# A four-stage attention and expert kernel on one core: stash copies in runs of four, a fixed matmul order for the first expert, weight loads on another queue

## The chip, the cores and the metric

The kernel runs on one core of a Trainium2 chip. The metric is device time in microseconds, the median of several executions. One execution was also profiled; its rows are what the text reads. The engines are named as in the profile: PE (matrix multiply) with PEld (its weight loads), DVE (vector), ACT (scalar), POOL (GpSimd) and SP (it issues DMAs). ACT and POOL can issue DMAs too; an issue stands in the engine's own instruction stream, in order. Each engine executes its instructions in the order in which the program laid them down; that order is decided before the run.

## What is computed

The reference chains three layers over 3072 tokens of width 384 (4 batches of 768 steps, 8 heads of 48).

```
for t in range(S):                      # gated linear attention, complex decay a
    S_re, S_im = a_t * (S_re, S_im) + (k_t v_t^T, 0)
    y_t = q_t @ S_re
e = argmax(x @ w_gate); do = x @ w_skip > 0
x = x + do * gate * relu(x @ w1[e]) @ w2[e]      # 8 experts, 384 -> 1024 -> 384
out = leaky(x @ w_in) @ w_out                    # 384 -> 2048 -> 384, leaky = max(0.01 h, h)
```

## The kernel before

The batches are handled in two halves, unit 0 and unit 1. For each unit the work has four parts.

**Rows.** `attention_rows` holds one sequence chunk of 96 steps in every partition row (128 rows: 2 batches, 8 heads, 8 chunks). It normalises `a` (`norm_pre`, `norm`), forms the running products `P` step by step on DVE (`steps`: one multiply into `t`, one add into `P`, each needing the last), and scales k and q by them (`scaled_pre`, `scaled`). Steps come in blocks (`BLKA` for unit 0, mostly 8 steps; `BLKB` for unit 1, mostly 6). For unit 0 the results stay in SBUF: `turned` transposes four steps of k or q at a time into one PSUM bank (`qkps`, 96 partitions by 4 steps by 128 rows) and ACT copies that bank into the `stash`, whose innermost dimension is the step. `timed` writes the order of DVE, ACT and PE in this part out by hand. A few ACT operations of the last blocks are given to POOL by the lists `GUARD_G` and `MIRROR_G`. For unit 1 the results go through a DRAM tensor `kqd`; this generator is called `behind` and is fed piecemeal into later parts.

**Chunks.** `attention_chunks` does scores, outputs and states per chunk on PE, then `Routing` selects 128 slots per expert.

**Experts.** `experts` runs eight experts for the unit. For each, `columns` transposes the gathered tokens, `first` does 48 matmuls into `hps` with four ReLUs (`hh`) on ACT, `second` does 16 matmuls into `yps`, and DVE adds (`xo`) before a scatter to `xd`. For unit 0 the weights are whole fp32 and lie in the stash: those of experts 0 to 3 come during the chunks, those of experts 4 to 7 by `fetch` into slots that an earlier expert's matmuls have finished reading. After each of the four groups of `first`, `go` calls `budget(behind, 2.0)` while `e < LASTE`: it emits background work (the generator `feed`) until its planned microseconds are used up, with DVE and ACT kept in program order. After expert 3's `first`, `swap` frees half of the stash and adds to `feed` the conversion of `w_in` (`convert`): 16 pieces, each loaded as raw 64-bit words (`raw`, two buffers), turned into fp32 on DVE (`cst`, three operations), split by ACT (high half, into `m2w`) and DVE (low half). `feed` takes one item from `behind` and one from the conversion in turn.

**Dense.** `Dense` does the two wide layers for 512 tokens at a time: `load` reads `xd` (tile `xr`), `columns` transposes, `first` gives `hps`, `second` gives `ops`. In the first of them the conversion of `w_out` runs as background work, in the next the rest of `behind`. Then unit 1 goes through chunks, experts and dense in the same way, with its expert weights converted to fp16 pairs.

Where nothing is kept in program order, a list scheduler orders the instructions of each engine by its own estimate of when they become ready.

Of the kernel before, what the change touches and what calls it, by code (L numbers as in the profile page):

```python
# [11 lines left out]
I32 = mybir.dt.int32  # L12
I64 = mybir.dt.int64
# [6 lines left out]
B, H, S, D = 4, 8, 768, 48  # L20
# [28 lines left out]
BG_START = 1.5  # L49
BG_CHUNK = 0.3  # L50
BG_ROUTE = 12.0
BG_EXPERT, LASTE = 2.0, 6
BG_DENSE = (1, 1.5, 1.5)
BG_WOUT = 0.3
BG_WSTART, BG_WEIGHT = 4.0, 0.35
# [11 lines left out]
SUM_NORM = (0, 1, 2)  # L67
SUM_SCALED = (12, 13)
MIRROR = (0, 1)
GUARD_G = (10, 11, 13)  # L70
MIRROR_G = (11, 12, 13)
LISTS = dict(sp=(0, 1), tp=(2, 3, 7), yps=(4,), ups=(5,), tr=(6,), bk=(7,))
DEEP = {"kqt": 3, "vt": 3, "qT": 3}
LISTSA = dict(sp=(0, 1), yps=(2,), ups=(3,), tr=(4, 5, 6), bk=(7,))
# [4 lines left out]
def moe_attention_kernel(ctx, tc, q, k, v, a_re, a_im, w_skip, w_gate, w1, w2, w_in, w_out, out,  # L79
                         cap=CAP):  # L80
    nc = tc.nc
# [13 lines left out]
    V, A, T, G = Engine(nc.vector, "V"), Engine(nc.scalar, "A"), Engine(nc.tensor, "T"), Engine(nc.gpsimd, "G")  # L95

    def keep(engines):
        for n in order:
            order[n] = n in engines
# [50 lines left out]
    def rows3(x):  # L150
        return x.rearrange("(k p) f -> p k f", p=128)


    def attention_rows(ui, ep, blks, sum_pe, queue, store, stash=None, more=None):
# [31 lines left out]
        a4s, Ps, ins, pre, turns, lags = {}, {}, {}, {}, [], []  # L186
# [24 lines left out]
        def norm_pre(i):  # L211
# [14 lines left out]
            A.activation(rr, r0, AF.Square)  # L226
            if stash and i in GUARD_G:
                G.tensor_scalar(s2, r0, 0.5e-6 / MAGCAP, -0.5, ALU.mult, ALU.add)
# [4 lines left out]
        def norm(i):  # L233
# [21 lines left out]
            for c in range(2):  # L255
                if stash and i in MIRROR_G and not c:
                    G.tensor_scalar(a4[:, :, 3 - 2 * c, :], a4[:, :, 2 * c, :], 1.0 - 2 * c, None, ALU.mult)
# [21 lines left out]
        def scaled(i):  # L279
# [30 lines left out]
            if stash:  # L310
                turns.append(turned(i, kq))
            else:
                queue.dma_start(kqd[t0s[i]:t0s[i] + blks[i]].rearrange("t r a d -> r t (a d)"),
                                kq[2].rearrange("r t a c d -> r t (a c d)"))
            yield cost(i, 2)

        def turned(i, kq):

            for g in range(0, blks[i], 4):
                m = min(4, blks[i] - g)  # L320
                for a in range(2):
                    p = ps.tile([2 * D, m, R], F32, tag="qk", name="qkps")
                    for j in range(m):
                        T.transpose(p[:, j, :], kq[a][:, g + j].rearrange("p c d -> p (c d)"), ident)
                    t = t0s[i] + g
                    lags.append((stash[a][:2 * D, :, :, t:t + m].rearrange("p c b t -> p t (c b)"), p))
                    if len(lags) > 1:
                        A.activation(*lags.pop(0), AF.Copy)
                    yield
# [461 lines left out]
    def convert(pool, src, hi, lo, scale, cut, shape, n):  # L791

        raw, t = {}, {}
        el = 1
        for d in shape:
            el *= d
        cost = (70 + 1.04 * el) / 1e3
        for j in range(n + 1):  # L800
            if j:
                A.activation(hi[cut(j - 1)], t[j - 1], AF.Copy, scale=scale)
            if j < n:
                r = pool.tile([128] + shape + [2], I32, tag="raw", name="raw")
                nc.sync.dma_start(r.rearrange("p k f w -> p k (f w)").bitcast(I64), rows3(src)[cut(j)])
                t[j] = pool.tile([128] + shape, I32, tag="cst", name="cst")
                V.tensor_scalar(t[j], r[:, :, :, 1], 0x07FFFFFF, 3, ALU.bitwise_and, ALU.logical_shift_left)
                yield 0.6 * cost
                V.scalar_tensor_tensor(t[j], r[:, :, :, 1], -0x40000000, t[j], ALU.bitwise_and, ALU.bitwise_or)
                yield cost  # L810
                V.scalar_tensor_tensor(t[j], r[:, :, :, 0], 29, t[j], ALU.logical_shift_right, ALU.bitwise_or)
                t[j] = t[j].bitcast(F32)
                yield cost
            else:
                yield 0.0
            if j:
                V.scalar_tensor_tensor(lo[cut(j - 1)], t[j - 1], scale, hi[cut(j - 1)], ALU.mult, ALU.subtract)
                yield cost
# [3 lines left out]
    def cut_columns(m, n):  # L822
        return lambda j: (al, al, slice(j * m // n, (j + 1) * m // n))

    def cut_rows(m, n):
        return lambda j: (al, slice(j * m // n, (j + 1) * m // n))
# [12 lines left out]
    class Experts:  # L839
# [2 lines left out]
            self.ui, self.whole, self.place = ui, whole, place  # L842
            self.w, self.xg, self.xt, self.h, self.slots, self.made = {}, {}, {}, {}, [], 0

        def weights(self, e, layer, half):

            src, k, m = ((w1[e], 3, F1), (w2[e], 8, DM))[layer]
            t = self.w[e, layer] = self.place(e, layer).rearrange("p (k m) -> p k m", k=k)
            c = (al, al, slice(half * m // 2, (half + 1) * m // 2)) if layer == 0 else \
                (al, slice(half * k // 2, (half + 1) * k // 2))  # L850
            nc.scalar.dma_start(t[c], rows3(src)[c])

        def part(self, i):

# [96 lines left out]
    class Dense:  # L951
# [4 lines left out]
        def load(self):  # L956
            self.xr = self.xp.tile([128, 4, DM], F32, tag="xr", name="xr", bufs=1)
            nc.sync.dma_start(self.xr, xd[self.ui][self.t * TN:(self.t + 1) * TN, :]
                              .rearrange("(s p) c -> p s c", p=128))
# [43 lines left out]
    def run(*gens):  # L1003
        for gen in gens:
            for _ in gen:
                pass
# [3 lines left out]
    def budget(gen, us, engines=""):  # L1010

        was = "".join(n for n in order if order[n])
        keep(engines)
        owed[0] += us
        while owed[0] > 0:
            x = next(gen, None)
            owed[0] = 0.0 if x is None else owed[0] - x
        keep(was)

    def later(us, gen):  # L1020

        for _ in range(int(us * 10)):
            yield 0.1
        for x in gen:
            yield x
# [127 lines left out]

    def experts(ex, behind, us, then={}, mixed=none):

        ex.columns(0)
        for e in range(E):
            gen = none if ex.place else ex.made_to(2 * e + NSLOT, ex.stage)
            if e in (() if ex.place else MIX):
                next(mixed, None)  # L1160

            def go():
                for _ in range(3):
                    next(gen, None)
                budget(behind, us if e < LASTE else 0.0, "VA")

            for _ in ex.first(e):
                go()
            then.get((e, 0), list)()
            if e + 1 < E:  # L1170
                ex.columns(e + 1)
            run(gen)
            ex.second(e)
            then.get((e, 1), list)()
# [7 lines left out]
    stash = [p.tile([128, NCH, HB * H, L], F32, name="stash") for p in blocks]  # L1182
# [25 lines left out]
    ex = Experts(0, range(E), place)  # L1208

    def fetch(*which):  # L1210
        def go():
            for e, layer in which:
                for half in range(2):
                    ex.weights(e, layer, half)
        return go

    chunks_and_routing(ck[0], rt, later(BG_START, behind), BG_CHUNK,
# [11 lines left out]
    feed = share(behind)  # L1229
    mlp2 = {}  # L1230

    def swap():
        blocks[1].release()
        wpm = mlp2["w"] = tc.alloc_tile_pool(name="wpm", bufs=1)
        mlp2["x"] = tc.alloc_tile_pool(name="m2x", bufs=2)
        cp = mlp2["c"] = tc.alloc_tile_pool(name="cp", bufs=2)
        for i, (shape, src, scale, cut, part) in enumerate((
                ([128, 3, F2], w_in, SWI, cut_columns(F2, CVP), [3, F2 // CVP]),
                ([128, 16, DM], w_out, SWO, cut_rows(16, CVP), [16 // CVP, DM]))):
            t = mlp2[i] = [wpm.tile(shape, F16, name=f"m2w{i}{j}") for j in range(2)]  # L1240
            mlp2["conv", i] = convert(cp, src, *t, scale, cut, part, CVP)
        feed.gens.append(mlp2["conv", 0])

    then = {(i // 2, i % 2): fetch((i // 2 + 2, i % 2)) for i in range(8, 12)}
    then.update({(i, 1): fetch((4 + i // 2, i % 2)) for i in range(4)})
    then[3, 0] = swap
    experts(ex, feed, BG_EXPERT, then=then)
    (wih, wil), (woh, wol), m2x = mlp2[0], mlp2[1], mlp2["x"]
    conv = mlp2["conv", 1]
# [22 lines left out]
    ex = Experts(1, ())  # L1272
# [5 lines left out]
    conv = later(BG_WSTART, ex.made_to(4, ex.stage))  # L1278
# [15 lines left out]
    conv = ex.made_to(NSLOT, ex.stage)  # L1294
# [3 lines left out]
    run(conv)  # L1298
    rest = second_ff(dense[ND:nd], True)
    experts(ex, none, 0.0, mixed=rest)  # L1300
    dense[nd].load()
    run(rest)
# [139 lines left out]
```

## Time and profile before

| | us |
|---|---|
| median of 3 runs | 952.55 (951.84 to 953.05) |
| the profiled execution | 956.44 |
| its span, first to last instruction | 954.0 |
| PE busy | 840.4 |
| DVE busy | 612.4 |
| ACT busy | 518.0 |
| POOL busy | 137.2 |

By the trace the parts of unit 0 lie at about 0 to 151 us (rows), 151 to 249 (chunks and routing), 249 to 372 (experts) and 372 to 514 (two dense tiles); unit 1 follows to the end. Busy shares are averages over parts with different limits, so the rows below are taken by stretch.

### The profile page before, as it was taken

To read this page: it belongs to the slowest core of one execution; us is meant where nothing else is said; L and a number is where in the kernel's file an instruction comes from. 1 tells how busy PE (TensorE), PEld (TensorE's weight loads), DVE (VectorE), ACT (ScalarE), POOL (GpSimd) and SP (SyncE) were. 2 spreads that over 40 slices of the span, in tenths; PEclk is the share of its full clock that TensorE was granted. 3 is DMA by queue.
4 is the path that set the end of the run, shared out by engine and by line. 5 is a ranking of instruction groups with operands and counts; after the bars stand their busy time and mean duration, and the time that the engine had idled before them with its cause. 6 is when DMAs were issued, how large, how long until landed. Compare 5 with 4: busy or idle time off the path is not lost.

```text
span 954.0 us, 17829 instructions
## 1 busy us (share of the span) xinstructions
PE 840.4 (88%) x6674; PEld 584.8 (61%) x6674; DVE 612.4 (64%) x1534; ACT 518.0 (54%) x1065; POOL 137.2 (14%) x168
## 2 busy tenths in 40 slices
PE   1787878899299783999999988999999999999997
PEld 1665667898288572455457978846776645546454
DVE  6978884677788579999961555587577262260430
ACT  4879896676255343654743867655566261350430
POOL 9100022221541012000012111140011000000000
PEclk9979897999599986999999989999999999999999
DMA  5555544898668876445246898242766201000000
GB/s 152 143 152 159 139 114 144 243 290 268 200 206 276 283 271 217 147 134 172 78 156 165 224 234 241 75 162 86 246 201 214 88 1 51 18 1 25 9 10 27
DMA packets 126512, 143.61 MB, mean 151 GB/s; under 512 B 34058, under 2 KB 109514, under 8 KB 126416
## 3 DMA queue, kind: packets, MB, share of 16 engines
q1 hardware_dynamic: 106064, 107.88, 38.5%
q10 hardware_dynamic: 18304, 29.89, 9.6%
q0 software_dynamic: 2048, 4.61, 1.4%
q8 instruction: 54, 0.88, 0.4%
q14 instruction: 42, 0.34, 0.1%
HBM read 115.62 MB, written 28.41 MB: 151 GB/s over the span
## 4 chain that ended last, share of the span: by engine, by line
PE 55%; DVE 16%; DMA 14%; ACT 10%; issue 3%; SPq 1%; ACTq 0%; POOL 0%; DVEq 0%; POOLq 0%
PE ops L91 17%; PE hps L91 13%; PE yps L91 7%; PE sps L91 4%; DVE gg L91 3%; DMA raw<-in_moe_w_in_dram 3%; DVE gl L91 3%; DVE cst L91 2%; PE ad L91 2%; ACT stash L91 2%; PE tps L91 2%; ACT gh L91 2%; DMA kqt<-kqd 2%; PE ups L91 2%; DMA cw<-in_moe_w_dram 2%
## 5 line engine op out<-in xcount | busy, mean ns | idle before, releaser
L91 PE MATMUL hps<-xTh,m2w 128*128 128x512 f16 x576 | 174.1, 381 | 0.6 <-issue 0.3
L91 PEld LDWEIGHTS <-m2w 128*128 128x128 f16 x864 | 84.5, 98 | 100.7 <-issue 3.9
L91 PE MATMUL ops<-m2w,gh 128*128 128x384 f16 x512 | 125.2, 326 | 0.0
L91 PE MATMUL hps<-xTl,m2w 128*128 128x512 f16 x288 | 109.4, 381 | 0.1
L91 DVE TENSOR_TENSOR gg<-hps,gg 128x512 f32<-128x512 f32 x96 | 65.8, 685 | 65.5 <-ACT gg L91 65.1
L91 PE MATMUL ops<-m2w,gl 128*128 128x384 f16 x256 | 83.5, 326 | 0.0
L91 ACT ACTIVATE ot<-ops 128x384 f32<-128x384 f32 x24 | 11.6, 489 | 121.2 <-PE ops L91 121.2
L91 PEld LDWEIGHTS <-gh 128*128 128x128 f16 x512 | 50.1, 98 | 32.7
L91 DVE TENSOR_TENSOR t<-P,a 128x192 f32<-128x192 f32 x190 | 66.8, 352 | 1.3 <-ACT a L91 0.4
L91 PE MATMUL ops<-m2w,stash 128*128 128x384 f16 x384 | 65.3, 326 | 1.8 <-ACT m2w L91 1.8
L91 ACT ACTIVATE gg<-hps 128x512 f32<-128x512 f32 x96 | 56.3, 586 | 17.5 <-PE hps L91 12.4
L91 DVE TENSOR_TENSOR gl<-gg,gh 128x512 f16<-128x512 f32 x64 | 44.2, 690 | 33.6 <-ACT gh L91 33.3
L91 DVE SCALAR_TENSOR_TENSOR w<-cw,w 128x768 f16<-128x768 f32 x64 | 59.8, 953 | 7.7 <-ACT w L91 7.2
L91 ACT ACTIVATE gh<-gg 128x512 f16<-128x512 f32 x64 | 40.3, 630 | 43.2 <-DVE gg L91 42.9
L91 ACT ACTIVATE w<-cw 128x768 f16<-128x768 f32 x64 | 53.0, 844 | 17.9 <-DMA cw<-in_moe_w_dram 15.4
L91 POOL TENSOR_SCALAR_AFFINE_SELECT sc<-sc 96x384 f32<-96x384 f32 x64 | 34.6, 550 | 157.6 <-ACT sc L91 157.2
L91 PEld LDWEIGHTS <-stash 128*128 128x128 f16 x384 | 37.5, 98 | 29.2 <-issue 4.8
L91 POOL DMA_INDIRECT xd<-xo,idx x16 | 25.2, 1574 | 179.9 <-DVE xo L91 166.1
L91 ACT ACTIVATE stash<-qkps 96x512 f32<-96x512 f32 (+1 forms) x50 | 50.0, 1025 | 0.4 <-PE qkps L91 0.4
L91 DVE TENSOR_TENSOR P<-t 128x96 f32<-128x96 f32 x190 | 48.5, 255 | 1.6
L91 PE MATMUL yps<-stash,hh 128*128 128x384 f32 x128 | 44.7, 503 | 3.8 <-ACT hh L91 3.8
L91 ACT ACTIVATE hh<-hps 128x256 f32<-128x256 f32 (+1 forms) x64 | 23.8, 378 | 40.6 <-PE hps L91 28.7
(245 smaller groups left out, 1779.6 us busy)
## 6 DMA issues: line engine op xcount, KB each, us to landing
stash<-in_moe_w_dram ACTq DMA_DIRECT2D x32, 768.0 KB
cw<-in_moe_w_dram SPq DMA_DIRECT2D x64, 384.0 KB
kqt<-kqd SPq DMA_DIRECT2D x16, 576.0 KB
kqd<-kq SPq DMA_DIRECT2D x14, 576.0 KB
vd<-gv SPq DMA_DIRECT2D x32, 192.0 KB
vt<-vd SPq DMA_DIRECT2D x32, 192.0 KB
raw<-in_moe_w_in_dram SPq DMA_DIRECT2D x16, 384.0 KB
raw<-in_moe_w_out_dram SPq DMA_DIRECT2D x16, 384.0 KB
```

What stands on the lines that cost most here:

```text
L91: ins = getattr(self.engine, op)(*args, **kw)
```

## The change

Six edits. The stash copies walk the bank with the step innermost, so that four consecutive stash elements are written one after another, and PSUM is read with a step of 128 elements. The lists that gave six operations to POOL are empty, so ACT does them. In `experts` of unit 0, PE keeps program order from the first expert's `columns` until the second's. The weights that `fetch` loads are issued by SP in place of ACT. `convert` issues the load of a piece before the work on the piece ahead of it, and the first load already in `swap`. The conversion of `w_in` now goes ahead of `behind` in the feed instead of in turn with it, and the background budget runs to expert 6 instead of expert 5.

```
-BG_EXPERT, LASTE = 2.0, 6
+BG_EXPERT, LASTE = 2.0, 7
-GUARD_G = (10, 11, 13)
-MIRROR_G = (11, 12, 13)
+GUARD_G = ()
+MIRROR_G = ()
...
-                    lags.append((stash[a][:2 * D, :, :, t:t + m].rearrange("p c b t -> p t (c b)"), p))
+                    lags.append((stash[a][:2 * D, :, :, t:t + m].rearrange("p c b t -> p (c b) t"),
+                                 p.rearrange("p t r -> p r t")))
...
+        def load(j):
+            raw[j] = pool.tile([128] + shape + [2], I32, tag="raw", name="raw")
+            nc.sync.dma_start(raw[j].rearrange("p k f w -> p k (f w)").bitcast(I64), rows3(src)[cut(j)])
+
+        load(0)
+        yield 0.0
         for j in range(n + 1):
+            if j + 1 < n:
+                load(j + 1)
             if j:
                 A.activation(hi[cut(j - 1)], t[j - 1], AF.Copy, scale=scale)
             if j < n:
-                r = pool.tile([128] + shape + [2], I32, tag="raw", name="raw")
-                nc.sync.dma_start(r.rearrange("p k f w -> p k (f w)").bitcast(I64), rows3(src)[cut(j)])
+                r = raw.pop(j)
...
-        def weights(self, e, layer, half):
+        def weights(self, e, layer, half, queue=nc.scalar):
...
-            nc.scalar.dma_start(t[c], rows3(src)[c])
+            queue.dma_start(t[c], rows3(src)[c])
...
+        if ex.place:
+            keep("T")
         ex.columns(0)
...
                 ex.columns(e + 1)
+            keep("")
             run(gen)
...
-                    ex.weights(e, layer, half)
+                    ex.weights(e, layer, half, nc.sync)
...
-        feed.gens.append(mlp2["conv", 0])
+        next(mlp2["conv", 0])
+        feed.gens = [first_of([mlp2["conv", 0]] + feed.gens)]
```

## Rows read from the trace of the kernel before

**Rows 1.** Windows: each engine's busy time (x instructions), granted clock, DMA share, GB/s.
```profile
90.00:120.00 30.00, 23.93 (x164) 18.18 (x162) 26.32 (x78) 26.83 (x54) 2.33 (x3) 0.89 0.55 142
...
301.00:320.00 19.00, 19.00 (x112) 14.71 (x111) 11.04 (x30) 8.66 (x22) 1.09 (x1) 1.00 0.99 321
```

**Rows 2.** Waits of DVE, 30 to 150 us: us in total, times, longest.
```profile
DVE pu L91 <- ACT pg L91: 16.1, 13, 3.5
```

**Rows 3.** Groups by form on ACT: busy and mean ns of one.
```profile
L91 ACT ACTIVATE stash<-qkps 96x512 f32<-96x512 f32 x46 | 47.9, 1062 | 0.0
...
L91 ACT ACTIVATE sT<-stp 96x512 f32<-96x512 f32 x28 | 16.6, 593 | 2.9 <-PE stp L91 2.7
```

**Rows 4.** Groups by form on DVE, both reading PSUM.
```profile
L91 DVE TENSOR_REDUCE LG<-xps 96x9 f32<-96x72 f32 x32 | 7.3, 228 | 47.5 <-ACT xrow L91 47.3
...
L91 DVE COPY sv<-bank 128x40 f32<-128x40 f32 x2 | 0.4, 194 | 0.6 <-PE bank L91 0.6
```

**Rows 5.** Timeline of PE and DVE around 100 us, two operations of one block.
```profile
98.54 2.93 PE L91 MATMUL ad<-psq,ident 128*128 128x384 f32 x4
...
102.64 0.56 DVE L91 TENSOR_TENSOR pu<-ad,pg 128x384 f32<-128x384 f32 x1 [2.78 <-ACT pg L91]
```

**Rows 6.** Groups by form on ACT: one kind that POOL shared.
```profile
L91 ACT ACTIVATE nsq<-nr 128x384 f32<-128x384 f32 x9 | 4.6, 508 | 0.0
```

**Rows 7.** Timeline of PE, 254 to 296 us: experts 0 to 2.
```profile
254.20 0.87 PE L91 MATMUL tp__3514<-ident,xg 128*128 128x128 f32 x3 [5.91 <-DVE nrr L91]
260.89 0.90 PE L91 MATMUL tp__3610<-ident,xg 128*128 128x128 f32 x3 [5.82 <-DMA xg<-xd,idx]
261.58 7.50 PE L91 MATMUL hps<-xT__3518,stash 128*128 128x128 f32 x48
...
285.26 5.52 PE L91 MATMUL hps<-xT__3726,stash 128*128 128x128 f32 x48
...
295.78 5.52 PE L91 MATMUL hps<-xT__3841,stash 128*128 128x128 f32 x48
```

**Rows 8.** Timeline of PE, from expert 4 to the first dense tile.
```profile
306.63 5.52 PE L91 MATMUL hps<-xT__3965,stash 128*128 128x128 f32 x48
...
334.73 8.52 PE L91 MATMUL hps<-xT__4174,stash 128*128 128x128 f32 x48 [4.87 <-ACT xT__4174 L91]
...
356.74 7.12 PE L91 MATMUL yps<-stash,hh 128*128 128x384 f32 x16 [2.98 <-ACT hh L91]
379.26 1.97 PE L91 MATMUL tp<-ident,xr 128*128 128x128 f32 x8 [15.40 <-DMA xr<-xd]
```

**Rows 9.** Waits of ACT, 301 to 380 us.
```profile
ACT m2w L91 <- DVE cst L91: 22.3, 9, 6.6
ACT hh L91 <- DMA stash<-in_moe_w_dram: 10.4, 2, 5.3
```

**Rows 10.** Timeline of SP, DVE and ACT, 310 to 367 us.
```profile
310.52 2.95 SPq L805 DMA_DIRECT2D raw<-in_moe_w_in_dram  x2
320.19 0.36 DVE L91 TENSOR_SCALAR cst<-raw 128x384 int32<-128x384 int32 x1 [5.80 <-DMA raw<-in_moe_w_in_dram]
...
334.26 5.35 ACTq L851 DMA_DIRECT2D stash<-in_moe_w_dram  x2
...
367.00 0.61 DVE L91 SCALAR_TENSOR_TENSOR xo<-yps,gsl,xg 128x384 f32<-128x384 f32 x1
```

**Rows 11.** DMA issues: tensor, queue, count, size of one.
```profile
stash<-in_moe_w_dram ACTq DMA_DIRECT2D x32, 768.0 KB
...
raw<-in_moe_w_in_dram SPq DMA_DIRECT2D x16, 384.0 KB
```

**Rows 12.** Waits in SP's queue, 241 to 446 us.
```profile
SPq L805 <- DVE cst L91: 52.1, 17, 7.9
```

**Rows 13.** SP's last store of kqd (timeline); unit 1's first chunk matmuls (chain).
```profile
495.12 0.36 SPq L313 DMA_DIRECT2D kqd<-kq  x1
...
513.51 3.16 PE tps L91 x32
```

## Prediction

> **What bounds the kernel now.** I read the windows first, then the waits, then the timeline where a wait named two suspects. PE is busy for 840 of 954 us, so only stretches where PE stands can give much. There are two in unit 0, and the change touches both.
>
> The first is the rows part. There neither DVE nor ACT is full but both are close: from 90 to 120 us DVE is busy 26.3 and ACT 26.8 of 30 [rows 1]. The recurrence on DVE sets the floor. What holds DVE up is in the waits: 16.1 us in 13 stops before `pu`, all put down to ACT's `pg` [rows 2]. The timeline shows two causes behind that name. In one block the stop is 2.8 us, and most of it lies behind the sum `ad` on PE, which alone takes 2.9 us [rows 5]; in others ACT's own queue is last. So about half of these stops are ACT's.
>
> The second is from the routing's end to the first dense tile. PE stands three times: before expert 0, in experts 5 to 7, and after the last expert. The timeline of PE gives each length.
>
> **The change, part by part.**
>
> *Stash copies.* A copy of 96x512 takes 1062 ns, 46 of them; a plain copy of as many elements from PSUM takes 593 ns [rows 3]. If the new order runs like the plain one, ACT is freed of 46 x 0.47 = 21.6 us. Of that the span gets at most what DVE waited for ACT, 16.1 us; at least nothing. I take 9, a little over half, since PE's sums remain. The write side is cured by construction (consecutive elements); the question is the read, which now steps 128 elements in PSUM. The nearest row is on DVE: a reduction that reads PSUM with a step of 64 elements takes 228 ns for 72 elements, a contiguous one 194 for 40 [rows 4]. The difference, 34 ns for 32 elements, is the ordinary price of one element each, so the step costs DVE nothing there. For ACT no row shows it. Bounds for the copy: 0.59 us, and 1.06 + 0.47 = 1.53 us if the read pays what the write paid and the write still does. I take 0.6, by the DVE row. The Trainium skill, Advanced Engine Details and Errata, Memory Cachelines, speaks against this edit: PSUM lines hold two fp32 values and steps between lines are slow, though it says so for matmuls; by it the copy would stay near 1.06 and this term would be nothing.
>
> *Six operations from POOL to ACT.* At most 0.5 us each [rows 6], some 2.2 us in all as they get smaller towards the end. The room that the copies free hides them; without that room they cost up to 2.2.
>
> *Expert 0 in written order.* The tokens of expert 0 are transposed at 254.2, but PE's next instruction is the transpose for expert 1, which waits until 260.9 for its gather; only then do expert 0's 48 matmuls start, at 261.6 [rows 7]. In written order they start when ACT has copied the transpose, about 255.9 (0.87 for the transpose, 0.5 for the copy, gaps). That is 5.7 earlier; the second transpose then adds its 0.7 after them. I take 5 (bounds 0 and 5.8). The wait for the second gather is late next, but it ends at 260.9, before the 7.5 us of matmuls are through.
>
> *Weights from SP, loads ahead, conversion first.* An undisturbed expert takes 295.78 - 285.26 = 10.5 us [rows 7]. Experts 4 to 7 run from 306.6 to 363.9, 57.2 us where four undisturbed ones take 42.1, with some 1.4 for transposes 43.5 [rows 8]: 13.7 us lost. ACT's waits say how: 22.3 us for a piece of `w_in` that DVE had not finished, 10.4 us held by a weight load that could not be issued yet [rows 9]; the ReLUs stand behind both in ACT's order, and PE behind the ReLUs. One weight issue alone held ACT for 5.4 us [rows 10]. On SP that hold disappears from ACT. What stands behind it there are the `raw` loads and the loads of `behind`; the latter are asked for two or three blocks ahead, so a hold of 5 us costs them nothing.
>
> The raw loads are another matter. SP already waits 52.1 us for DVE to give a `raw` buffer back [rows 12], so the loads were as early as two buffers allow, and the load-ahead is worth nothing by itself. What made DVE stand was the transfer: issued at 310.5, usable at 320.2 [rows 10], while DMA was 0.99 busy at 321 GB/s [rows 1]. So I price by bytes. While experts 4 to 6 run, five weight layers of two 768 KB loads and about 11 pieces of 384 KB must come [rows 11]: 7.9 + 4.3 = 12.2 MB, 38 us at 321 GB/s, against 31.6 us of undisturbed matmuls. 6.4 us of the 13.7 stay; I take a gain of 7 (bounds 0 and 13.7).
>
> *After the last expert.* Its matmuls end at 363.9, but DVE, busy with late conversion, adds at 367.0 [rows 8, 10]; the scatter, the reload and the transposes follow, at 379.3. With 13 of 16 pieces planned before expert 7 (24 us of budget at 1.8 a piece) instead of 4, DVE should be free: 3 (bounds 0 and 4).
>
> *What is paid back.* `behind` gives up its share in experts 4 and 5, one block of six steps, about 7 us of DVE, to the dense tiles. PE sets the pace there; `behind` stored its last rows at 495.1 and unit 1's chunks began at 513.5 [rows 13], 18.4 us apart. If I allow for the first load between them the 9.7 us of the crowded raw transfer [rows 10], 8.7 us remain and cover the 7. If the experts gain more than DVE does, up to 5 us of it shows as a wait there. I take 0.
>
> Sum: 9 + 5 + 7 + 3 = 24. The profiled execution took 956.4 and would take 932.4; it lies 3.9 above the median, so the median goes to 952.55 - 24 = 928.5.
>
> **Rivals.**
>
> *The sum holds:* 928.5, with its own range 918 to 939. Chance 0.50.
>
> *Bandwidth keeps the stalls.* Weights and pieces now share one queue, and a piece waits for the two halves in front of it, 1.6 MB or 5 us. Then the 7 us are not gained: 935.5. For it speaks the 0.99 [rows 1]; against it, that ACT is then no longer the one that is held. Chance 0.16.
>
> *The copies do not get quicker.* Read step for write step: 9 lost and 2 paid, 939.5. Against it stands the DVE row alone. The rule that the Trainium skill states on memory cachelines would give this. Chance 0.13. If the copy even goes to 1.53, ACT has 21.6 us more, nearly all of which shows since it is 0.89 busy: 24 - 9 - 20 gives 957.5; chance 0.04.
>
> *All waits go.* 16.1 + 5.8 + 13.7 + 4 = 39.6 gives 913. Chance 0.08.
>
> *The other side: the conversion holds the ReLUs.* Thirteen pieces instead of four now stand, in fixed order, among the ReLUs of experts 4 to 6. When raw loads share DMA with weights, two pieces took 320.2 - 310.5 = 9.7 us, 4.8 each. At that pace 13 pieces take 62 us where 31.6 are wanted: 31 lost instead of 13.7, so this term is -17 instead of +7, and the 5 us of chunk wait come too: 9 + 5 - 17 + 3 - 5 = -5, 957.5. It decides from 4.5 us a piece on. Against it: 12.2 MB do not fill 62 us. Chance 0.09.
>
> **How the numbers follow.** Predicted: 928.5. The cases from 915 to 944 hold a little over 0.8 (half of the case at 913, all of the three in the middle), so that is the range. A run to run spread of 1.2 us on 952 makes 0.2%, 1.9 us, about the least that can be told from no change. Faster: 0.50 + 0.16 + 0.13 + 0.08 = 0.87. The two slow cases have 0.13, of which 0.03 fall within 0.2% and 0.10 beyond.
>
> **What would show it.** The `stash<-qkps` form at about 600 ns, and DVE's wait for `pg` halved. The first `hps` of the experts straight behind its transpose, and no wait of PE for `xg` before it. No ACT row idle because of `stash<-in_moe_w`, and the experts from 4 to 7 in about 50 us; `cst` on DVE still waiting for `raw`. The tail from the last `yps` to `tp` at 12 us. Unit 1's chunks starting without a wait for `kqt`. The forecast is wrong if the copies stay above 0.9 us, if experts 4 to 6 take over 45 us, or if PE stands before unit 1's first `tps`.

## The result, and the profile after

The changed kernel takes 924.24 us (919.73 to 924.88, four runs) where the kernel before took 952.58 beside it: ratio 0.9695, 95% interval 0.9668 to 0.9722, 28.3 us less. The forecast was 928.5, a gain of 24. The profiled execution took 919.73, span 917.6. It lies 4.5 us under its median and that of before 3.9 over its own, so the two profiles differ by 36.4, some 8 more than the medians, and the parts below overstate the gain by as much in all. By parts of the two traces, cut at PE's first instruction of each:

| part | before | after | change | forecast |
|---|---|---|---|---|
| rows, to the first `kps` | 150.96 | 134.71 | -16.25 | -9 |
| chunks and routing, to expert 0's `tp` | 103.24 | 103.94 | +0.7 | 0 |
| expert 0's `tp` to its `hps` | 7.38 | 1.45 | -5.9 | -5 |
| experts 0 to 3 | 45.05 | 44.90 | -0.15 | 0 |
| experts 4 to 7, to the last `yps` | 57.2 | 43.5 | -13.7 | -7 |
| to the first dense `tp` | 15.4 | 17.8 | +2.4 | -3 |
| first two dense tiles | 134.2 | 134.4 | +0.2 | 0 |
| unit 1 from its first `tps` | 440.5 | 436.9 | -3.6 | 0 |

The rows part first. These are the windows of the changed kernel (same columns as [rows 1]); the line of the kernel before for the same stretch follows.

```profile
60.00:90.00 30.00, 25.35 (x187) 19.10 (x187) 29.55 (x88) 27.07 (x64) 0.00 (x0) 1.00 0.66 185
90.00:120.00 30.00, 24.64 (x185) 19.16 (x183) 26.93 (x84) 24.61 (x64) 0.00 (x0) 0.94 0.59 154
```

```profile
60.00:90.00 30.00, 25.26 (x155) 18.65 (x154) 24.45 (x73) 26.18 (x52) 0.00 (x0) 0.83 0.58 155
```

From 60 to 90 us DVE is now busy for 29.55 of 30 us: it does 88 instructions where it did 73, so the recurrence runs nearly without a stop there. The granted clock of PE, the column before the DMA share, is 1.00 where it was 0.83. The waits of DVE from 30 to 150 us and the groups by form on ACT answer to [rows 2] and [rows 3]:

```profile
DVE pu L91 <- ACT pg L91: 4.1, 5, 1.2
```

```profile
L91 ACT ACTIVATE stash<-qkps 96x512 f32<-96x512 f32 x46 | 26.5, 584 | 0.0
L91 ACT ACTIVATE sT<-stp 96x512 f32<-96x512 f32 x28 | 16.6, 592 | 2.9 <-PE stp L91 2.7
```

A copy takes 584 ns, what a contiguous one takes, and the stops before `pu` have gone from 16.1 us to 4.1. The timeline of PE from expert 0 on answers to [rows 7, 8, 13]:

```profile
238.65 0.87 PE L91 MATMUL tp__3514<-ident,xg 128*128 128x128 f32 x3 [5.85 <-DVE nrr L91]
240.10 7.03 PE L91 MATMUL hps<-xT__3518,stash 128*128 128x128 f32 x48 [0.58 <-ACT xT__3518 L91]
246.97 0.49 PE L91 MATMUL tp__3610<-ident,xg 128*128 128x128 f32 x3
...
285.00 5.52 PE L91 MATMUL hps<-xT__3967,stash 128*128 128x128 f32 x48
...
322.90 5.56 PE L91 MATMUL yps<-stash,hh 128*128 128x384 f32 x16
346.26 1.97 PE L91 MATMUL tp<-ident,xr 128*128 128x128 f32 x8 [17.80 <-DMA xr<-xd]
```

Unit 1's first `tps`, in the chain that ended last:

```profile
480.70 3.16 PE tps L91 x32
```

Expert 0 starts right behind its own transpose. The rows of experts 4 to 7 have no bracket, the idle time before a row, and unit 1's chunks follow the second dense tile at the old distance. The window of experts 4 to 7 and ACT's waits from 280 to 346 us say how (the latter answer to [rows 9]):

```profile
285.00:328.50 43.50, 43.46 (x266) 34.31 (x264) 41.14 (x112) 20.33 (x50) 17.39 (x4) 1.00 0.95 320
```

```profile
ACT m2w L91 <- DVE cst L91: 8.7, 8, 2.5
ACT a L91 <- DVE a L91: 7.0, 3, 3.2
ACT psq L91 <- DVE P L91: 6.5, 2, 4.2
ACT nsq L91 <- DMA ari<-in_a_im_dram: 5.3, 2, 3.6
ACT hh L91 <- PE hps L91: 2.1, 3, 1.1
```

PE is busy 43.46 of 43.50 us, so it never waits there, with DMA 0.95 busy at 320 GB/s for the whole stretch. `hh` no longer waits for a weight load, and ACT waits for `cst` 8.7 us in place of 22.3. DVE, busy 41.1 of 43.5, is now the fullest engine beside PE, and the timeline of the tail shows what that costs:

```profile
333.94 0.55 DVE L91 SCALAR_TENSOR_TENSOR cst<-raw,cst 128x384 int32<-128x384 int32 x1
334.41 0.61 DVE L91 SCALAR_TENSOR_TENSOR xo<-yps,gsl,xg 128x384 f32<-128x384 f32 x1
...
335.29 4.35 POOL L91 DMA_INDIRECT xd<-xo,idx  x1 [10.93 <-DVE xo L91]
...
341.78 0.37 SPq L966 DMA_DIRECT2D xr<-xd  x1
```

The last `yps` ends at 328.5, and the add that needs it starts at 334.4, behind other work in DVE's order: 6 us late where it was 3 late before.

### The profile page after: what moved, and what is told of

It reads as the page before. It is cut to its first block, busy times and chain, and to the rows that moved or that the text cites. A ratio compares the mean times of both kernels' runs of the same rounds, so it can differ in the third digit from the quotient of the medians.

```text
span 917.6 us, 17826 instructions
## 1 busy us (share of the span) xinstructions
PE 820.6 (89%) x6674; PEld 569.8 (62%) x6674; DVE 608.4 (66%) x1534; ACT 502.4 (55%) x1071; POOL 140.5 (15%) x162
## 4 chain that ended last, share of the span: by engine, by line
PE 52%; DVE 18%; DMA 15%; ACT 10%; issue 3%; SPq 1%; ACTq 0%; POOLq 0%; POOL 0%; DVEq 0%
PE ops L91 18%; PE hps L91 12%; PE yps L91 6%; PE sps L91 4%; DVE gg L91 4%; PE ad L91 3%; DVE cst L91 3%; DVE gl L91 3%; DMA cw<-in_moe_w_dram 2%; ACT gh L91 2%; PE tps L91 2%; DMA raw<-in_moe_w_in_dram 2%; DMA kqt<-kqd 2%; DMA vt<-vd 2%; PE ups L91 2%
## 5 line engine op out<-in xcount | busy, mean ns | idle before, releaser
L91 DVE TENSOR_TENSOR gl<-gg,gh 128x512 f16<-128x512 f32 x64 | 44.2, 690 | 33.9 <-ACT gh L91 33.2
L91 ACT ACTIVATE w<-cw 128x768 f16<-128x768 f32 x64 | 53.0, 842 | 18.6 <-DMA cw<-in_moe_w_dram 16.1
L91 POOL DMA_INDIRECT xd<-xo,idx x16 | 35.3, 2204 | 155.0 <-DVE xo L91 113.0
L91 PE MATMUL yps<-stash,hh 128*128 128x384 f32 x128 | 42.8, 487 | 0.0
L91 PE MATMUL yps<-sc,vt 128*64 128x96 f32 x512 | 41.6, 251 | 0.0
```

Of the source, the lines that this page charges most:

```text
L91: ins = getattr(self.engine, op)(*args, **kw)
```

## The experiments

Each ran five rounds beside the kernel before. "Ratio" is to that kernel, with its 95% interval.

**The changed kernel again.** No edit.

> The changed kernel once more, as the mark for the three beside it: 924, 0.9695 of the kernel before, within 2 us. If the gain of the rows part in its profile (16.3 us) was partly a luckier execution of the profile, this run's profile shows the first chunk matmul later than 134.7 us; if it was the copies, it shows it at 134 to 136.

926.02 us, ratio 0.9707 (0.9663 to 0.975). First `kps` at 136.7, later than in the first profile, and experts 4 to 7 in 45.5 us, not 43.5. The same rows part stands, unedited, in five further kernels below and ended between 132.7 and 139.3; so a profile tells the length of that part to some 3 us either way.

**Copies alone**, on the kernel before.

```
-   stash[...].rearrange("p c b t -> p t (c b)"), p
+   stash[...].rearrange("p c b t -> p (c b) t"), p.rearrange("p t r -> p r t")
```

> The kernel before with the stash copies alone. Theory: ACT's freed time (46 copies at 0.58 in place of 1.06, 22 us) reaches the span by what DVE waited for ACT: 9 to 16 us, so 936 to 944, with DVE's wait for pg under 6 us and copies near 585 ns. Rival 1, PE's clock in the rows part (0.83 in the profile of before, 1.00 after) made most of it: under 5 us, 948 or more, with the wait for pg still above 10. Rival 2, the copies release more than the waits held, since ACT's chain of the next block also starts earlier: over 16, below 936.

937.5, ratio 0.9842 (0.9799 to 0.9884): 14.0 us less. First `kps` at 131.4. DVE's wait for `pg` and, by form on PE from 30 to 130 us, the sums `ad`, in the kernel before and in this one:

```profile
DVE pu L91 <- ACT pg L91: 0.8, 3, 0.3
```

```profile
L91 PE MATMUL ad<-psq,ident 128*128 128x384 f32 x36 | 20.0, 690 | 2.9 <-ACT psq L91 2.3
```

```profile
L91 PE MATMUL ad<-psq,ident 128*128 128x384 f32 x36 | 14.9, 538 | 4.6 <-ACT psq L91 4.6
```

**Old copies in the changed kernel**, the same two lines the other way.

> The changed kernel with the old copies; the six small operations stay on ACT. Theory: the mirror of the copies alone, plus up to 2.2 us for the six operations that now have no room: 9 to 18 us over the changed kernel, 933 to 942, with the wait for pg at 16 us or more. Rival (clock): under 5 us more, 929 or less. If the loss is more than 18, the six operations on a full ACT cost more than their own length.

936.09, ratio 0.9813 (0.9768 to 0.9859): 10.1 more than the changed kernel beside it. First `kps` at 152.2. The same two views:

```profile
DVE pu L91 <- ACT pg L91: 17.8, 11, 2.8
```

```profile
L91 PE MATMUL ad<-psq,ident 128*128 128x384 f32 x32 | 20.1, 774 | 2.0 <-ACT psq L91 1.4
```

The copies are worth 10 to 14 us by the times, 15.5 by the rows parts of all profiles (three with old copies end at 148.9 to 152.2, mean 150.7; eleven with new ones at 131.4 to 139.3, mean 135.2). The clock is not a cause apart from the edit: from 30 to 120 us its mean was 0.85, 0.79 and 0.86 in the three kernels with old copies, and 0.94 to 1.00 in all eleven with new ones; between the kernel before and the copies alone nothing else was edited. The mean sum on PE fell as the clock rose, from 690 ns to 538.

But part of the gain comes by way of the clock. In one stretch, the kernel with the weights on SP alone (below) ran old copies at a granted 1.00:

```profile
60.00:90.00 30.00, 23.34 (x174) 17.47 (x175) 27.46 (x81) 28.93 (x59) 0.00 (x0) 1.00 0.64 171
```

DVE was idle for 2.5 us there, for 5.6 in the kernel before at 0.83 and for 0.5 with new copies at 1.00. So in this stretch some 3 of the 5.1 us go with the clock and 2 with shorter copies at the same clock. By which path shorter copies raise the clock no run shows.

**Six operations back on POOL**, in the changed kernel.

```
-GUARD_G = ()
-MIRROR_G = ()
+GUARD_G = (10, 11, 13)
+MIRROR_G = (11, 12, 13)
```

> The changed kernel with the six operations back on POOL. Theory: ACT has room since the copies are short, so they cost nothing there: within 1.5 us of the changed kernel. Rival: POOL's operations are longer than ACT's and late, and giving them to ACT was part of the gain in the rows part: 3 us or more over the changed kernel.

919.21, ratio 0.9658 (0.9611 to 0.9705): 6.8 less than the changed kernel beside it, the wait for `pg` 1.0 us, first `kps` at 133.3. Neither the theory's 1.5 us nor the rival's loss came. So the edit to ACT is no gain, and may be a loss; the intervals overlap. The clock is an open rival: in this profile it was 1.00 from 30 to 120 us, in that of the changed kernel beside it 0.94.

**First expert not in written order.**

```
-        if ex.place:
-            keep("T")
         ex.columns(0)
...
-            keep("")
```

> The changed kernel without the written order for the first expert. Theory: PE takes the transpose for expert 1 first again and waits for its gather; expert 0 starts 5 to 6 us later and nothing makes that up: 929 to 930. Rival: the time comes back later, in the tail after the last expert (17.8 us between the last matmul and the first dense transpose, while DVE finishes late conversion), since background work gets the same 6 us: 925 or less, with that tail near 12.

929.0, ratio 0.9739 (0.9684 to 0.9795): 3 to 5 more than the two runs of the changed kernel. The timeline of PE is the old one again:

```profile
241.49 0.88 PE L91 MATMUL tp__3514<-ident,xg 128*128 128x128 f32 x3 [5.84 <-DVE nrr L91]
248.22 0.90 PE L91 MATMUL tp__3610<-ident,xg 128*128 128x128 f32 x3 [5.86 <-DMA xg<-xd,idx]
```

The tail was 16.8, so nothing came back there.

**Weights on ACT's queue**, in the changed kernel.

```
-                    ex.weights(e, layer, half, nc.sync)
+                    ex.weights(e, layer, half)
```

> The changed kernel with the weights of experts 4 to 7 issued by ACT again. Theory of the prediction (ACT held by an issue is one half of the stalls): experts 4 to 7 lose 5 to 10 us more, 929 to 934, with ACT rows idle because of stash<-in_moe_w. Rival 1, the queue did not matter because the early loads and the feed order took the stalls away: within 2 us of the changed kernel. Rival 2, all of the stalls came with it: 937 or more.

941.21, ratio 0.9855 (0.9806 to 0.9904): 14 to 17 more (the ratios give the 14), the whole of the stalls and more. Experts 4 to 7 take 62.5 us, longer than before the change; the tail is 13.5. Its windows there, ACT's waits, and the timeline of one stall:

```profile
291.00:354.00 63.00, 49.58 (x266) 37.98 (x265) 39.88 (x95) 19.62 (x50) 9.77 (x4) 0.89 0.75 245
302.00:306.00 4.00, 0.48 (x4) 0.24 (x2) 0.19 (x1) 0.00 (x0) 0.00 (x0) 0.92 0.92 342
306.00:310.00 4.00, 1.07 (x5) 1.07 (x6) 4.00 (x11) 0.90 (x2) 0.00 (x0) 0.50 0.25 46
```

```profile
ACT m2w L91 <- DVE cst L91: 46.1, 18, 10.3
```

```profile
305.81 0.36 DVE L91 TENSOR_SCALAR cst<-raw 128x384 int32<-128x384 int32 x1 [7.46 <-DMA raw<-in_moe_w_in_dram]
...
307.97 0.52 ACT L91 ACTIVATE m2w<-cst 128x384 f16<-128x384 f32 x1 [10.26 <-DVE cst L91]
308.04 0.37 ACTq L859 DMA_DIRECT2D stash<-in_moe_w_dram  x1
...
308.40 0.47 ACT L91 ACTIVATE xT__4062<-tp__4058 128x384 f32<-128x384 f32 x1
...
308.93 7.15 PE L91 MATMUL hps<-xT__4062,stash 128*128 128x128 f32 x48 [6.45 <-ACT xT__4062 L91]
```

From 302 to 306 us DMA is 0.92 busy, and the piece that DVE waits for is among what comes. Then the rate falls to 46 GB/s, because the next weight load stands behind `m2w` in ACT's order and `m2w` waits for that piece: while ACT waits, no weights are asked for, and PE waits for `xT` behind both. DMA moves 245 GB/s over the stretch, not 320.

**Weights on SP alone**, on the kernel before: `queue=nc.scalar` and `queue.dma_start` in `weights`, `nc.sync` in `fetch`, no other edit.

> The kernel before with the weights of experts 4 to 7 on SP's queue and nothing else. Theory (ACT, held by a weight load or by m2w, kept back the next weight load, so that DMA stood still between bursts): all 13.7 us of the stalls go and nothing else moves, 937 to 940, with experts 4 to 7 in 43.5 to 45 and the DMA share near 0.95 there. Rival 1, that of the prediction: bandwidth keeps half, 944 to 947. Rival 2, the queue needs the early load or the conversion first beside it: under 4 us gained, 948 or more.

943.96, ratio 0.9906 (0.9873 to 0.994): 9.4 less. In its window of experts 4 to 7 PE is busy 44.0 of 45.6 us:

```profile
303.70:349.30 45.60, 44.04 (x266) 34.16 (x264) 33.73 (x88) 20.43 (x52) 10.88 (x4) 1.00 0.93 302
```

Of the 13.7 us of stalls 11.7 are gone with this edit alone; the tail is 17.7, 2.3 longer, and the two come to the 9.4. The time alone would not decide: it lies outside the theory's 937 to 940, at the edge of the rival's 944 to 947. The trace does, since PE hardly stands and DMA is 0.93 busy; what the theory missed is the longer tail.

**Loads in place**, in the changed kernel: no `load(0)` ahead, `load(j)` where the piece's work stands.

> The changed kernel with each piece loaded where its work stands, as before. Theory of the prediction: worth nothing by itself, since SP waited for DVE to free a raw buffer: within 1.5 us of the changed kernel, the same waits of DVE for raw. Rival: with the weights on SP too, a load that stands late falls behind two weight halves (5 us at 320 GB/s), and the stalls of experts 5 to 7 return: 3 to 7 us more, 927 to 931.

923.97, ratio 0.9693 (0.9643 to 0.9744). Nothing, as predicted.

**Conversion in turn with `behind`**, budget to expert 5, in the changed kernel.

```
-BG_EXPERT, LASTE = 2.0, 7
+BG_EXPERT, LASTE = 2.0, 6
...
-        feed.gens = [first_of([mlp2["conv", 0]] + feed.gens)]
+        feed.gens.append(mlp2["conv", 0])
```

> The changed kernel with conversion and behind in turn and the budget only to expert 5, as before. In the built order the DVE rows are much alike with and without it: at expert 7's add 10 pieces are through here, 11 in the changed kernel, because steps of behind that are issued in the dense part are not kept in order and stand between the pieces. Theory from that: within 2 us of the changed kernel. Rival, that of the prediction: the order matters, the tail after the last expert is 3 us longer or experts 5 to 7 stall again: 927 or more.

921.26, ratio 0.9657 (0.9608 to 0.9707). No loss without the edit; it took 3 us less, within the intervals. Experts 4 to 7 take 44.4 us and the tail 14.8.

**`behind` kept in order in the dense part**, in the changed kernel.

```
-        budget(behind, BG_DENSE[layer])
+        budget(behind, BG_DENSE[layer], "VA")
```

> The changed kernel with the steps of behind that the dense part issues held in program order on DVE and ACT, so that they can't be placed ahead among the pieces of the conversion: 142 steps of the recurrence stand before expert 7's add in place of 161, and 13 pieces are through in place of 11. Theory 1: DVE is then free when the last expert's matmuls end, and the tail goes from 17 to about 12: 918 to 921, if the dense part takes the 19 steps (some 25 us of DVE). Rival, what the prediction put at nothing: behind is late, and unit 1's chunks wait for it by what exceeds the 8.7 us of margin, up to 16 us: 930 to 938, with PE standing before unit 1's first tps.

960.22, ratio 1.0085 (1.0054 to 1.0117): 34 to 36 us more than the changed kernel, beyond the rival's 938 too. The tail fell to 14.2, and PE's waits from 300 to 520 us show the price:

```profile
PE tps L91 <- DMA kqt<-kqd: 36.4, 1, 36.4
PE tp L91 <- DMA xr<-xd: 14.2, 1, 14.2
```

Unit 1's chunks wait 36.4 us for rows that `behind` had not stored. `xo` was still 5 us late in the tail, behind pieces of the conversion alone.

**Three edits**, on the kernel before: the copies, the first expert's order, the weights on SP; each as above.

> The kernel before with three of the six edits: the stash copies, the written order for the first expert, and the weights on SP. The lists of POOL, the place of the loads, the turn of conversion and behind stay as before. Theory from the single runs: the lists on POOL are worth 4 to 6 us (rows part), conversion in turn 0 to 4 (tail after the last expert 14.8 in place of 17), the load in place 0; so 914 to 920, with the first transpose of expert 0 near 236.5, experts 4 to 7 in 44, the tail at 15. Rival: those two differences were from one execution to the next, 922 or more.

924.2, ratio 0.9701 (0.9658 to 0.9743). The same as all six. Experts 4 to 7 take 44.2 us in its trace, but the tail 18.6, against the expectation. These three carry the whole gain, as far as the interval tells.

**POOL's lists and conversion in turn together**, in the changed kernel.

> The changed kernel with the six operations back on POOL and with conversion and behind in turn again (budget to expert 5): the two edits whose removal gave the lowest times, together. If both differences are of the kernel, they add: 4 us in the rows part (first chunk matmul at 131 to 133 us) and 0 to 2 in the tail, 914 to 919. If they are from one execution to the next, as the version with three edits suggests (it lacks only the early loads beside this one and took 924.2), 921 to 925.

918.76, ratio 0.9628 (0.9578 to 0.9678): 6.4 us under the changed kernel by the ratios (0.0067, with an interval of 0.0057 either side when the two are put together), so just outside what the measurement can't tell. But its profile does not show it in the rows part: its first `kps` came at 138.2, not 131 to 133. Its tail was 13.7, the shortest of all with the weights on SP, where that of the three edits, with conversion in turn too, was 18.6. This kernel has only the loads ahead more than the three edits, and taking those back changed nothing above; yet the two lie 5.4 us apart. So a difference of this size can come between kernels without a cause that was found.

## Why the prediction came out

The time was within 4.3 us of the forecast, and the likeliest case, the sum, is the one that held. Inside it, terms went wrong in both directions, so that the total came so close is partly luck: copies and experts gave more than their terms, and the tail took where it was to give.

*Stash copies: 9 forecast, 10 to 14 measured.* The copy took the price it was given (0.6, measured 0.584). The step that failed is "a little over half, since PE's sums remain": they did not remain as they were. The sum in [rows 5], four matmuls in 2.9 us, ran at a granted clock of 0.50; the same four in the next block, at 1.00, took 1.56 us:

```profile
110.15 1.56 PE L91 MATMUL ad<-psq,ident 128*128 128x384 f32 x4 [0.58 <-ACT psq L91]
```

With the new copies the clock was higher and the mean sum fell from 690 to 538 ns, so nearly all of the 16.1 us could go (0.8 is left with the copies alone). The Trainium skill, Advanced Engine Details and Errata, Memory Cachelines, says of matmuls that PSUM reads which are not contiguous slow them down; carried over to ACT, as the prediction tried, it would have kept the copy near 1.06 us. Here ACT read PSUM in steps of 128 elements at 584 ns, so for ACT it doesn't hold.

*Six operations: 0 forecast.* The reasoning was by capacity: ACT has room, so they are hidden. Their removal gave 919.2 beside 926.0, with less wait for `pg` (1.0 in place of 4.0 us), which speaks for some microseconds lost. The last run, with the lists and yet a rows part of 138.2 us, speaks against it, and so does the clock, which differed too. Whether the edit costs anything stays open.

*Expert 0: 5 forecast, 3 to 5 measured,* 5.9 in the trace. Right, and nothing gave it back.

*Experts 4 to 7: 7 forecast, 13.7 in the trace, 11.7 with the queue alone.* The step that failed is that 12.2 MB "must come" while experts 4 to 6 run. The rate held, the amount did not: in the changed kernel experts 4 to 6 took 32.5 us at 328 GB/s, 10.7 MB, and PE did not stand.

```profile
285.00:317.50 32.50, 32.50 (x202) 26.18 (x201) 31.14 (x86) 16.43 (x40) 16.42 (x3) 1.00 0.97 328
```

The pieces beyond that came later, and no instruction of PE there needed them. Nor was DMA full for the stretch in the kernel before; it was full in bursts. Its own windows, and the rows that end the two pauses:

```profile
330.00:334.00 4.00, 0.00 (x0) 0.00 (x0) 2.83 (x8) 0.52 (x1) 0.00 (x0) 1.00 0.22 78
350.00:354.00 4.00, 3.77 (x34) 3.57 (x32) 3.57 (x9) 0.00 (x0) 0.00 (x0) 1.00 0.27 96
```

```profile
333.13 0.52 ACT L91 ACTIVATE m2w<-cst 128x384 f16<-128x384 f32 x1 [5.56 <-DVE cst L91]
333.14 1.00 ACTq L851 DMA_DIRECT2D stash<-in_moe_w_dram  x2
...
350.43 0.76 DVE L91 TENSOR_TENSOR kq<-kq,P 128x576 f32<-128x576 f32 x1 [5.21 <-DMA kqd<-kq]
...
354.09 0.90 SPq L805 DMA_DIRECT2D raw<-in_moe_w_in_dram  x2
```

The 0.99 in [rows 1] was one burst of 19 us. Between bursts 78 and 96 GB/s were moved. In the first pause the next weight loads stood in ACT's order behind an `m2w` that waited. In the second no weight load was left: DVE, which runs in a fixed order, had stood 5.2 us for a store of `behind`, and SP's next piece waited for the buffer that DVE had not given back. Of ACT's two waits, "held by a weight load" and "waiting for a piece", the queue was the key to both: with the loads on SP the transfers run at 320 GB/s all through, 13.9 MB in 43.5 us, and the pieces come in time. Moving the loads alone removed 11.7 us; taking only that edit back cost 14 to 17. The rival of bandwidth falls. The rival of the other side, conversion that holds the ReLUs, came in part in the one kernel that put the conversion first but left the weights on ACT: 62.5 us for experts 4 to 7 where 57.2 stood before, 19 lost where it priced 31.

*Loads ahead: 0 forecast, 0 measured,* with and without it 924.

*Conversion first: the step "13 of 16 pieces planned before expert 7 instead of 4" failed.* In DVE's order, by the traces, 12 pieces are through before expert 7's add in the kernel before and 11 in the changed one. Steps of `behind` that the dense part issues are not kept in order, and the scheduler places them ahead, among the pieces: 161 steps of the recurrence stand before that add in the changed kernel, 156 in the one before, 142 when they are kept in order.

*After the last expert: -3 forecast, +2.4 in the trace.* The experts now end earlier while DVE still has its work, and the add is 6 us late. The tail was 13.7 to 18.6 in ten other traces with the weights on SP, 13.5 to 15.4 in the three with them on ACT. In all fourteen traces the add starts 2.2 to 6.3 us after the last `yps`. Not all of the tail's spread is that: the add was 4.4 us late both with a tail of 13.5 and with one of 13.7, and 4.2 late with one of 16.9.

*Paid back in unit 1: 0 forecast, 0 measured, for another reason than given.* The margin of 8.7 us that was to cover it is not what covers it. `behind` was not deferred at all, since its steps were placed ahead; where they were held back (19 steps, not the prediction's block of six), 36.4 us of wait came at the very place that was named.

*Unit 1's 3.6 us* are in no step. The same part took 435.9 to 439.4 us in eleven of the twelve other traces (441.8 in that with `behind` kept in order), and none of the edits is in it, so this is put down to the execution.

In sum, by the times of single edits on the kernel before or taken back: 10 to 14 for the copies, 9.4 for the queue on the kernel before, 3 to 5 for the first expert make 23 to 28 of the 28.3, and the three together gave all of it. The other three edits are not needed for it.

## What to carry to other kernels

A DMA queued on an engine that also waits for data turns every wait into a stop of the transfers behind it. A window that is full then says little, so read short windows, and look for the empty ones, before pricing by bytes; and count only the bytes that must be there by then. Before work is called deferred, look where the scheduler may place it: what no order holds is moved into any gap, and it fills the engine that the next critical step needs.

## What was not expected of the hardware

ACT read PSUM in steps of 128 elements (512 bytes) at 584 ns for 96x512, no slower than a contiguous read (592), while writing SBUF with the old stride cost 1062. And the granted clock of TensorE followed an edit on another engine: 0.85 to 0.98 from 30 to 120 us (2.4 GHz throughout would be 1, stretches at 1.2 pull it down). PE was busy for 25.3 of 30 us from 60 to 90 us in the kernel before and 25.4 in the changed one, but with 155 instructions there and 187 here.
